# adaLN block on one core: the second part of the modulation vector summed by GpSimd during units 8 to 11

## The chip, the cores and the metric

The kernel runs on one core of a Trainium2 chip. A core has TensorE (matmuls, in the profile PE, its weight loads PEld), VectorE (DVE), ScalarE (ACT), GpSimd (POOL) and SyncE (SP, which here only issues DMAs); each works through its own queue of instructions in order, and they wait for each other by semaphores. SBUF is the on-chip memory of 128 partitions, PSUM the memory that TensorE writes to. The metric is the device time of one execution in microseconds (us).

## The reference

One transformer block with adaptive layer norm: 2048 tokens of width 448, 16 heads of 28, an MLP of 1792. A vector of six times 448 numbers, the modulation, is computed from the condition c and scales and shifts the two layer norms and the two branches:

```python
x = A_x
mod = (_silu(c) @ w_mod).reshape(c.shape[0], 6, 1, -1)
sa, ca, ga, sb, cb, gb = (mod[:, 0], mod[:, 1], mod[:, 2], mod[:, 3], mod[:, 4], mod[:, 5])
h = _layernorm(x, axis=-1) * (1 + ca) + sa
x = x + ga * _A_ref(h, A_wqkv, A_wo)      # softmax attention over 16 heads
h = _layernorm(x, axis=-1) * (1 + cb) + sb
x = x + gb * _B_ref(h, B_w1, B_b1, B_w2, B_b2)   # layer norm, GELU MLP
```

sa and ca are needed at once, for the first layer norm. The other four, ga, sb, cb and gb (called the second part of the modulation here), are needed late: ga scales the output weights of the attention, cb and sb the second layer norm, gb the MLP's second weights and its bias b2.

## The kernel before

Everything is float32; matmuls that must be exact are made of products of a high and a low half in the fp32r type. The work goes in three stages.

**First phase.** Blocks of 512 tokens (b = 0 to 3) go through the layer norm, transposes and the products for q, k and v. For each block a list of tasks runs (the loop at L830, index n within block b): q and k by groups of four heads, then v. Beside the tasks the kernel computes the row maxima of the scores that softmax needs: one matmul into a PSUM tile and one VectorE reduction over 512 columns each (`max_one`, the reduction at L481). The second part of the modulation stands in this phase. `mod_load` loads a chunk k of w_mod's rows (k = 0 to 2 of 128 rows, k = 3 of 64), 1792 columns wide, to the slots v2 and v3: k 0 and 1 in block 0, task 6, k 2 and 3 in block 1, tasks 0 and 1. `mod_mm` (block 1, tasks 0 to 3) multiplies it on TensorE by the silu of c: four matmuls per k, one for each 448 columns, each with 32 output rows that are all alike. `mod_fin` copies the four results out of PSUM (ScalarE, one of the copies adds 1 for cb), writes them to DRAM and loads them back, spread over all partitions, as the four rows `rows["ga"]`, `"sb"`, `"cb"` and `"gb"`.

**Second phase: 16 units of 16 steps.** A unit is one group g of four heads and one block qt of 512 queries (u = 4 g + qt, so units 8 to 11 are group 2); a step is 128 keys. The loop at L1311 writes the order of every engine's instructions out by hand. A step has twelve score matmuls (L1348) in two halves, two exponentials on ScalarE (L1361), four matmuls of probabilities by values (`av`, L1303), and beside them the row maxima of a later group. From step 121 on (`RING`) three PSUM tiles for scores go round, and the maxima of a step are one single, in the only tile left for it (m1, reduction L481), and one pair, in the score tile that is just unused (reduction L686). At the end of a step whatever the table `sched` holds for it is issued: `at(step, fn)` appends to a list, so what was put in earlier is issued earlier.

After each unit, `unit_end_tasks` divides its result by the softmax sums. For a unit u with base = 16 (u + 1) and the tasks marked `staged` (all that matter here): `t_den` at base + 1 (a DMA), `t_rec` at base + 4 (VectorE's reciprocal, a DMA to DRAM and a DMA back, spread over partitions, to the tile osb), `t_split` at base + 10 (GpSimd multiplies, L1061) and `t_split2` at base + 11 (VectorE casts the high half, L1071, GpSimd subtracts the low half, L1072, and eight DMAs store both). The tuple `times` has these offsets counted from base + 1. At each unit's third step `load_q` fetches the queries of the next unit; `load_hi` fetches q and k of a later group for the maxima, and `put` stores the maxima of a unit into its queries (L528). All of these DMAs stand in one queue, SyncE's.

In unit 0 `wo_prep` prepares the attention's output weights: it loads five pieces (`wo_item`), GpSimd multiplies each by `rows["ga"]`, VectorE casts the high half (L986, L981) and GpSimd subtracts. b2 is loaded at step 15 and multiplied by `rows["gb"]` at step 28. The results are first used by the projections in steps 8 to 11 of units 13 and 14.

**Third stage.** The MLP, with the second layer norm inside.

The names that the change touches: `cst` (a small tile of constants), `mod_load`, `mod_mm`, `mod_fin`, `wo_item`'s `rest` (the second half of a piece, put into `sched`), and the entries of `sched` for `wo_prep` and b2. The slots a2h, a3h and b1h are halves of larger slots that are free in the second phase until attention results are loaded into them at the end of unit 12 (`load_o`).

Of the kernel before, what the change touches and what calls it, by code (L numbers as in the profile page):

```python
# [13 lines left out]
F32 = mybir.dt.float32  # L14
F32R = mybir.dt.float32r
AF = mybir.ActivationFunctionType
ALU = mybir.AluOpType
# [15 lines left out]
P1RATE = 4  # L33
LAST_MAX = NKT - 4
RING = 121
PAIR_AT = (2, 2, 0, 2)
PAIR_ROWS = {(0, 2): 2, (0, 3): 3, (1, 0): 2, (1, 1): 2, (1, 2): 3}
WO_MAX = 3
# [6 lines left out]
def tile_adaln_block(ctx: ExitStack, tc: tile.TileContext, x, wqkv, wo, w1, b1, w2, b2, c, w_mod, out):  # L45
# [33 lines left out]
    def sbt(tag, shape, dt=F32, bufs=1):  # L79
        return sb.tile(shape, dt, tag=tag, name=nm(tag), bufs=bufs)  # L80

    def slot(tag, shape, dt=F32R):
        return sb.tile(shape, dt, tag="slot_" + tag, name=nm("slot_" + tag), bufs=1)
# [28 lines left out]
    def ps_o():  # L112
        return ps_tile("o")
# [7 lines left out]

    ident = sbt("ident", [128, 128])
    make_identity(nc, ident)
    cst = sbt("cst", [128, 5])
    neg_half, zero_col = cst[:, 0:4], cst[:, 4:5]
    pool.memset(neg_half, -0.5)
    pool.memset(zero_col, 0.0)


    cols = sbt("cols", [128, 2 * NC])  # L130
# [178 lines left out]
    def warm_up(n):  # L309
        for _ in range(n):  # L310
            pe.matmul(warm[:, :128], ident, ident, start=True, stop=True)
# [2 lines left out]
    pc = ps_o()  # L314
    pe.transpose(pc[:, :NC], c_rows, ident[:NC, :NC])
    act.activation(sil_b, pc[:, :NC, None].broadcast_to([128, NC, 32]), AF.Silu)
    warm_up(5)
    for k in range(NC):
        for j in range(2):
# [418 lines left out]

    mod = {}

    def mod_load(k):
        mod[k] = slot(f"v{2 + k % 2}", [128, 4 * D], F32)
        load_mod(mod[k], k, 2 * D, 4)

    def mod_mm(k):
        if k == 0:
            mod["p"] = ps_o()
        p = mod["p"]
        for j in range(4):
            rs_, cs = mod_part(k, j, 4)  # L750
            pe.matmul(
                p[32 * j : 32 * j + 32, :D], sil_b[rs_, k, :], mod[k][rs_, cs],
                start=(k == 0), stop=(k == NC - 1),
            )

    def mod_fin():
        t = sbt("full", [128, 512], bufs=3)
        act.copy(t[0:64, :D], mod["p"][0:64, :D])
        act.activation(t[64:96, :D], mod["p"][64:96, :D], AF.Identity, bias=1.0)
        act.copy(t[96:128, :D], mod["p"][96:128, :D])  # L760
        sp.dma_start(drow, t[0:128:32, :D])
        for j, name in enumerate(("ga", "sb", "cb", "gb")):
            t = sbt("row_" + ("b2g" if name == "ga" else name), [128, D])
            sp.dma_start(t, drow[j][None].broadcast_to([128, D]))
            rows[name] = t
# [51 lines left out]
    for b in range(NB):  # L817
# [12 lines left out]
        for n, (tb, kind, g) in enumerate(tasks):  # L830
# [41 lines left out]
                    later[n - 7](None)  # L872
            if n == (4 if b else 6):
                v_init(b)
            if b == 0 and n == 6:
                mod_load(0)
                mod_load(1)
            if b == 1 and n == 8:
                put_last_rows()
            if b == 2 and n == 5:  # L880
                sp.dma_start(b1_col, b1.rearrange("(k p) -> p k", p=128))
            if b == 1:
                if n < 2:
                    mod_mm(n)
                    mod_load(2 + n)
                elif n in (2, 3):
                    mod_mm(n)
                    if n == 3:
                        mod_fin()
            if not more:  # L890
                if n == 0:
                    load_q(0)
# [68 lines left out]
    def wo_item(n):  # L961
        def ld(r):
            if n == 4:
                pool.memset(r[:, :D], 0.0)
                for j in range(4):
                    sp.dma_start(r[32 * j : 32 * j + DH, :D], wo[NP + DH * j : NP + DH * j + DH, :])
                return
            p0 = 0
            for r0, r1 in (((128 * n, 128 * n + 128),), MIX_HI, MIX_LO)[max(0, n - 1)]:
                sp.dma_start(r[p0 : p0 + r1 - r0, :D], wo[r0:r1, :])  # L970
                p0 += r1 - r0

        def go(r):
            full = sbt("full", [128, 512], bufs=3)
            ps = slice(0, 112 if n == 3 else 128)
            pool.tensor_tensor(out=full[ps, :D], in0=r[ps, :D], in1=rows["ga"][ps], op=ALU.mult)

            def rest():
                if n == 3:
                    hi = sbt("hi", [128, 512], F32R, bufs=3)  # L980
                    dve.tensor_copy(hi[ps, :D], full[ps, :D])  # L981
                    pool.tensor_tensor(out=wo_p[1][ps, 2, :], in0=full[ps, :D], in1=f(hi)[ps, :D], op=ALU.subtract)
                    pool.tensor_copy(wo_p[1][0:32, 2, :], f(hi)[0:32, :D])
                    return
                k = min(n, 3)
                dve.tensor_copy(wo_p[0][:, k, :], full[:, :D])  # L986
                if n != 2:
                    pool.tensor_tensor(out=wo_p[1][:, k, :], in0=full[:, :D], in1=f(wo_p[0])[:, k, :], op=ALU.subtract)

            at(6 + 2 * n, rest)  # L990

        return ld, go

# [224 lines left out]
        sched.setdefault(step, []).append(fn)  # L1218

    wo_prep = Prep([wo_item(n) for n in range(5)])  # L1220
    at(0, lambda: wo_prep.load(2))
    for n in range(5):
        at(4 + 2 * n, wo_prep.step)

    def b2_load():
        rows["b2"] = raw_t()
# [13 lines left out]
        at(1 + i, lambda: put_spare(1))  # L1240
    for g in (1, 2):
        at(6 + g, lambda g=g: put_ones(g))
    at(15, b2_load)
    at(28, b2_mul)
    last0 = NKT * (NU - 1)
    lnst = [ln2_stages(b) for b in range(NB)]
    for i in range(14):
# [257 lines left out]
```

## Time and profile before

| | |
|---|---|
| time, median of 3 runs | 1103.45 us (1102.35 to 1103.99) |
| time of the profiled execution | 1103.82 us |
| its span, first to last instruction | 1101.7 us |
| granted TensorE clock | 1.00 |
| DMA | 82.67 MB, mean 75 GB/s |

In the profiled execution the first phase takes the time until about 167 us, the 16 units go on until about 792 us, and the MLP fills the rest. Steps of the second phase take some 2.3 us each from step 121 on. A row of an engine in order of time reads: start and length in us, engine, line, operation, output<-inputs, shape, how many were merged, and in brackets how long the engine was idle before and what ended that. A grouped row has line, engine, operation, shapes, count, then busy us and mean ns. "28*128" before a matmul's shape is rows and columns of TensorE's array in use. fp32 matmuls of `mod_mm` and `av` appear as two records each.

### The profile page before, as it was taken

The numbers are of one execution on the slowest core, as the hardware profiler recorded it, in microseconds if no ns is written. First come the engines' busy times: TensorE is split into PE (matmuls) and PEld (weight loads), VectorE is DVE, ScalarE is ACT, GpSimd is POOL, SyncE is SP. The second block draws the span as 40 slices with busy tenths as digits, with TensorE's granted clock in tenths as the row PEclk, the third lists the DMA queues.
The fourth block names the chain that finished last, engine by engine and source line by source line (L and its number), as shares of the span: only waits on it lengthen the run. The fifth ranks groups of instructions, "written<-read, shape, count | busy, mean of one in ns | idle before, by whom it ended". The sixth has DMA issues, their size and how long they took to land.

```text
span 1101.7 us, 20731 instructions
## 1 busy us (share of the span) xinstructions
PE 1094.3 (99%) x8303; PEld 665.3 (60%) x8303; DVE 798.9 (73%) x1382; ACT 697.3 (63%) x883; POOL 196.8 (18%) x201
## 2 busy tenths in 40 slices
PE   9999999999999999999999999999999999999998
PEld 6756675444444444444444444554488888888887
DVE  6968788999999989988888888574655644444322
ACT  4655667888888888888888888678933411211210
POOL 1543332210000000000000000116123214023000
PEclk9999999999999999999999999999999999999999
DMA  9553354221222201231211313111451000000000
GB/s 311 199 191 106 99 183 138 60 64 33 75 76 61 76 28 40 69 102 47 69 48 38 98 42 99 57 31 59 146 144 50 27 34 1 15 20 1 34 1 34
DMA packets 51094, 82.67 MB, mean 75 GB/s; under 512 B 13327, under 2 KB 19878, under 8 KB 50986
## 3 DMA queue, kind: packets, MB, share of 16 engines
q1 hardware_dynamic: 50514, 80.61, 23.9%
q8 instruction: 65, 1.06, 0.4%
q10 hardware_dynamic: 148, 0.46, 0.1%
q0 software_dynamic: 336, 0.28, 0.1%
q14 instruction: 31, 0.25, 0.1%
HBM read 56.25 MB, written 26.75 MB: 75 GB/s over the span
## 4 chain that ended last, share of the span: by engine, by line
PE 97%; DVE 1%; ACT 0%; DMA 0%; issue 0%; ACTq 0%; DVEq 0%
PE s L1348 23%; PE o L1303 23%; PE m L396 17%; PE pa L396 9%; PE m L476 8%; PE s L1439 3%; PE s L1440 3%; PE s L1438 3%; PE s L476 2%; PE t L1439 1%; PE t L1440 1%; PE t L1438 1%; PE o L277 1%; DVE mxp L481 0%; PE ma L476 0%; PE m L277 0%
## 5 line engine op out<-in xcount | busy, mean ns | idle before, releaser
L481 DVE TENSOR_REDUCE mxp<-m 128x1 f32<-128x512 f32 x555 | 359.9, 686 | 64.7 <-PE m L476 46.9
L1348 PE MATMUL s<-slot_b,slot_a 28*128 28x512 f32 (+1 forms) x3072 | 356.7, 423 | 0.0
L1348 PEld LDWEIGHTS s<-slot_b,slot_a 28*128 28x128 f32 (+1 forms) x3072 | 211.2, 183 | 175.8 <-ACT slot_c L1361 96.4
L476 PE MATMUL m<-kh,qh 28*128 28x512 f32 x607 | 227.0, 468 | 0.4 <-DVE mxp L481 0.3
L1361 ACT ACTIVATE slot_c<-s 128x1024 f32<-128x1024 f32 x170 | 174.8, 1028 | 51.5 <-PE s L1348 50.8
L1303 PE MATMUL o<-slot_c,v 128*32 128x512 f32 x680 | 178.9, 605 | 0.0
L1394 ACT ACTIVATE full<-m,b_col 128x512 f32<-128x512 f32 x56 | 38.6, 689 | 205.3 <-PE m L396 188.5
L686 DVE TENSOR_REDUCE mxp<-s 128x2 f32<-128x1024 f32 x107 | 131.2, 1226 | 5.0
L1303 PE MATMUL o<-slot_c1h,v 128*32 128x512 f32 x512 | 134.7, 605 | 0.0
L1303 PE MATMUL o<-slot_c0h,v 128*32 128x512 f32 x508 | 133.6, 605 | 0.0
L1361 ACT ACTIVATE slot_c1h<-s 128x1024 f32<-128x1024 f32 x128 | 130.7, 1021 | 0.0
L1361 ACT ACTIVATE slot_c0h<-s 128x1024 f32<-128x1024 f32 x127 | 130.5, 1027 | 0.0
L1397 DVE CAST hi<-full 128x512 fp32r<-128x512 f32 x42 | 18.6, 443 | 121.1 <-ACT full L1394 121.1
L1361 ACT ACTIVATE slot_d<-s 128x1024 f32<-128x1024 f32 x86 | 88.4, 1028 | 25.2 <-PE s L1348 24.9
L476 PEld LDWEIGHTS m<-kh,qh 28*128 28x128 f32 x607 | 90.8, 182 | 15.2 <-DVE mxp L481 13.3
L1303 PE MATMUL o<-slot_d,v 128*32 128x512 f32 x344 | 90.5, 605 | 0.4 <-ACT osb L1267 0.4
L1061 POOL TENSOR_TENSOR osb<-osb,osb 128x512 f32<-128x512 f32 x16 | 20.6, 1284 | 363.5 <-DMA osb<-drec 247.1
L1398 DVE TENSOR_TENSOR lo<-full,hi 128x512 fp32r<-128x512 f32 x56 | 43.0, 768 | 26.6 <-ACT hi L1397 22.6
L396 PE MATMUL m<-y,slot_a 128*128 128x512 f32 x160 | 60.7, 395 | 0.0
L481 DVE TENSOR_REDUCE mxp<-ma 128x1 f32<-128x512 f32 x61 | 39.5, 682 | 13.2 <-PE m L476 8.0
L1303 PEld LDWEIGHTS o<-slot_c,v 128*32 128x32 f32 x680 | 24.5, 108 | 39.0 <-issue 36.4
L650 DVE CUSTOM_DVE_ANT_0 slot_d0i<-m,slot_d0i 128x512 f32<-128x512 f32 x54 | 37.3, 691 | 14.3 <-PE m L476 11.6
(351 smaller groups left out, 1835.7 us busy)
## 6 DMA issues: line engine op xcount, KB each, us to landing
slot_b<-d SPq DMA_DIRECT2D x32, 256.0 KB
slot_a<-d SPq DMA_DIRECT2D x32, 256.0 KB
d<-lo SPq DMA_DIRECT2D x28, 256.0 KB
d<-hi SPq DMA_DIRECT2D x16, 256.0 KB
osb<-drec SPq DMA_DIRECT2D x15, 256.0 KB
out_dram<-xn SPq DMA_DIRECT2D x16, 224.0 KB
raw<-in_B_w_dram SPq DMA_DIRECT2D x14, 224.0 KB
qh<-d SPq DMA_DIRECT2D x12, 256.0 KB
```

What stands on the lines that cost most here:

```text
L396: pe.matmul(p, a, b, start=(i == 0), stop=(i == len(terms) - 1))
L476: pe.matmul(m, qh_sb[(g, qt)][js, i * 128 : (i + 1) * 128], k[js, :], start=True, stop=True)
L481: dve.tensor_reduce(out=mxp[(g, qt)][:, i, j, cch : cch + 1], in_=m, op=ALU.max, axis=AX.X)
L686: dve.tensor_reduce(out=mxp[(g, qt)][:, i, j : j + 2, cch], in_=t, op=ALU.max, axis=AX.X)
L1303: pe.matmul(o[32 * j : 32 * j + 32, :], v_sb[kt // 4][:, kt % 4, 4 * g + j, :], p[j // 2][:, j % 2, :], start=(kt == 0), stop=(kt == NKT - 1),
L1348: pe.matmul(s2[:, jj, :], ks[rows_, kp, kc], qs[rows_, qp, :], start=(term == 0), stop=(term == 2))
L1361: act.activation(pt[hf], s2, AF.Exp, scale=SCALE)
L1394: act.activation(gf, p, AF.Gelu_apprx_tanh, bias=b1_col[:, i : i + 1])
L1398: dve.tensor_tensor(out=glo, in0=gf, in1=f(ghi), op=ALU.subtract)
L1438: pe.matmul(pp, ghi[:, ts], w_hi, start=(m == 0), stop=False)
L1439: pe.matmul(pp, ghi[:, ts], w_lo, start=False, stop=False)
L1440: pe.matmul(pp, glo[:, ts], w_hi, start=False, stop=(m == NFT - 1))
```

## The change

The second part of the modulation is no longer computed in the first phase. It is cut into two halves h of 896 columns (ga and sb; cb and gb). From step 130 on, every third step, one chunk k of one half is loaded to the slot a2h, which is the only buffer; two steps later GpSimd multiplies it by the column of silu(c) that belongs to its rows, and adds it to a running total (b1h for the first half, a3h for the second) unless it is the first. So there are eight loads, eight products and six additions, at steps 130 to 153. At step 156 the new `mod_fin` adds each total over the partitions by four matmuls with a weight of ones, taken from the ones column that v_sb holds anyway, copies the result out of PSUM in one ScalarE instruction whose bias `third` adds 1 on partitions 64 to 95 (cb), and goes on as before through DRAM. The rows that were in units 0 and 1 and need ga or gb move: the output weights to steps 162 to 176, b2's load to 177 and its product to 190.

```diff
+MOD_AT = 130
+WO_AT = 166
...
-    cst = sbt("cst", [128, 5])
-    neg_half, zero_col = cst[:, 0:4], cst[:, 4:5]
+    cst = sbt("cst", [128, 6])
+    neg_half, zero_col, third = cst[:, 0:4], cst[:, 4:5], cst[:, 5:6]
     pool.memset(neg_half, -0.5)
-    pool.memset(zero_col, 0.0)
+    pool.memset(cst[:, 4:6], 0.0)
+    pool.memset(third[64:96], 1.0)
+    sil_c = sbt("sil_c", [128, NC])
...
     act.activation(sil_b, pc[:, :NC, None].broadcast_to([128, NC, 32]), AF.Silu)
+    act.activation(sil_c, pc[:, :NC], AF.Silu)
...
-    def mod_load(k):
-        mod[k] = slot(f"v{2 + k % 2}", [128, 4 * D], F32)
-        load_mod(mod[k], k, 2 * D, 4)
-
-    def mod_mm(k):
+    def mod_rows(h, k):
+        return slice(0, 128) if k < 3 else slice(64 * h, 64 * h + 64)
+
+    def mod_load(h, k):
+        rs_ = mod_rows(h, k)
+        mod["raw"] = slot("a2h", [128, 2 * D], F32)
+        c0 = 2 * D * (1 + h)
+        sp.dma_start(mod["raw"][rs_], w_mod[128 * k : min(128 * k + 128, D), c0 : c0 + 2 * D])
+
+    def mod_add(h, k):
+        rs_ = mod_rows(h, k)
         if k == 0:
-            mod["p"] = ps_o()
-        p = mod["p"]
+            mod[h] = slot(("b1h", "a3h")[h], [128, 2 * D], F32)
+        raw, total = mod["raw"][rs_], mod[h][rs_]
+        col = sil_c[rs_, k : k + 1].broadcast_to([rs_.stop - rs_.start, 2 * D])
+        pool.tensor_tensor(out=raw if k else total, in0=raw, in1=col, op=ALU.mult)
+        if k:
+            pool.tensor_tensor(out=total, in0=total, in1=raw, op=ALU.add)
+
+    def mod_fin():
+        p = ps_mx()
+        ones_ = v_sb[0].rearrange("p t h d -> p (t h) d")[:, 0:32, DH]
         for j in range(4):
-            rs_, cs = mod_part(k, j, 4)
             pe.matmul(
-                p[32 * j : 32 * j + 32, :D], sil_b[rs_, k, :], mod[k][rs_, cs],
-                start=(k == 0), stop=(k == NC - 1),
+                p[32 * j : 32 * j + 32, :D], ones_, mod[j // 2][:, j % 2 * D : (j % 2 + 1) * D], start=True, stop=True,
             )
-
-    def mod_fin():
         t = sbt("full", [128, 512], bufs=3)
-        act.copy(t[0:64, :D], mod["p"][0:64, :D])
-        act.activation(t[64:96, :D], mod["p"][64:96, :D], AF.Identity, bias=1.0)
-        act.copy(t[96:128, :D], mod["p"][96:128, :D])
+        act.activation(t[:, :D], p[:, :D], AF.Identity, bias=third)
         sp.dma_start(drow, t[0:128:32, :D])
...
-            if b == 0 and n == 6:
-                mod_load(0)
-                mod_load(1)
...
-            if b == 1:
-                if n < 2:
-                    mod_mm(n)
-                    mod_load(2 + n)
-                elif n in (2, 3):
-                    mod_mm(n)
-                    if n == 3:
-                        mod_fin()
...
-            at(6 + 2 * n, rest)
+            at(WO_AT + 2 + 2 * n, rest)
...
-    at(0, lambda: wo_prep.load(2))
+    for i in range(2 * NC):
+        h, k = divmod(i, NC)
+        at(MOD_AT + 3 * i, lambda h=h, k=k: mod_load(h, k))
+        at(MOD_AT + 3 * i + 2, lambda h=h, k=k: mod_add(h, k))
+    at(MOD_AT + 6 * NC + 2, mod_fin)
+    at(WO_AT - 4, lambda: wo_prep.load(2))
     for n in range(5):
-        at(4 + 2 * n, wo_prep.step)
+        at(WO_AT + 2 * n, wo_prep.step)
...
-    at(15, b2_load)
-    at(28, b2_mul)
+    at(WO_AT + 11, b2_load)
+    at(WO_AT + 24, b2_mul)
```

## The prediction

> **What bounds the kernel now.** I read the page first (busy time, the chain that ended last), then the busy time of stretches, then the engines in order of time around each place that the change touches.
>
> ```profile
> PE 1094.3 (99%) x8303; PEld 665.3 (60%) x8303; DVE 798.9 (73%) x1382; ACT 697.3 (63%) x883; POOL 196.8 (18%) x201
> ...
> PE 97%; DVE 1%; ACT 0%; DMA 0%; issue 0%; ACTq 0%; DVEq 0%
> ```
>
> TensorE is busy 99% of the span and holds 97% of the chain. So a matmul taken out is worth its time, unless another engine is close behind, and any wait that TensorE newly meets is paid in full. GpSimd, at 18%, looks free. The stretches show who is close behind (the columns are the length, then PE, PEld, DVE, ACT, POOL busy):
>
> ```profile
> 65.00:75.00 10.00, 10.00 (x55) 5.52 (x54) 7.18 (x15) 5.70 (x12) 2.57 (x2) 1.00 0.82 274
> 520.00:560.00 40.00, 40.00 (x414) 17.16 (x410) 35.00 (x41) 34.80 (x38) 2.58 (x2) 1.00 0.21 59
> ```
>
> In the first phase, where matmuls leave, VectorE has 2.8 us of 10 to spare. In units 8 and 9 it has only 5 of 40, an eighth: VectorE there can't be late by much before TensorE is. The granted clock is 1.00 in both.
>
> **Removed: the first phase's matmuls.** TensorE in order of time, at the first and the last of the four calls of `mod_mm`:
>
> ```profile
> 58.34 0.96 PE L751 MATMUL o<-slot_v,slot_d 128*32 128x448 f32 x8
> 59.23 1.20 PE L396 MATMUL pa<-slot_c,slot_a 128*128 128x512 f32 x4
> ...
> 72.94 0.96 PE L751 MATMUL o<-slot_v,slot_d 64*32 64x448 f32 x8
> 73.82 1.20 PE L396 MATMUL pa<-slot_c,slot_a 128*128 128x512 f32 x4
> ```
>
> The next matmul starts 0.89 us after the first of a call, so the four hold TensorE for 4 x 0.89 = 3.55 us. How much comes back depends on VectorE, whose idle times there are the brackets:
>
> ```profile
> 61.12 1.89 DVE L481 TENSOR_REDUCE mxp<-m 128x1 f32<-128x512 f32 x3 [5.10 <-PE ma L476]
> ...
> 67.70 0.69 DVE L481 TENSOR_REDUCE mxp<-ma 128x1 f32<-128x512 f32 x1 [2.30 <-PE m L476]
> ...
> 70.56 1.29 DVE L481 TENSOR_REDUCE mxp<-ma 128x1 f32<-128x512 f32 x2 [0.37 <-PE m L476]
> ...
> 77.12 0.69 DVE L481 TENSOR_REDUCE mxp<-m 128x1 f32<-128x512 f32 x1 [2.27 <-PE ma L476]
> ```
>
> One idle time is only 0.37 us, less than the 0.89 taken out ahead of it; there TensorE waits about 0.5 us for a PSUM tile. The others are long enough. I take **-3.0 us**; ends -3.55 and, if VectorE's backlog takes it all, 0. ScalarE's three copies out of PSUM and SyncE's five DMAs of the old `mod_fin` go too. ScalarE is busy 5.70 us in 10 and nothing waited for those rows, so they count nothing.
>
> **Added at the start.** The small Silu for `sil_c` follows L316 on ScalarE. Its next instruction comes after an idle time that hides a fraction of a microsecond, so nothing:
>
> ```profile
> 8.34 0.76 ACT L233 ACTIVATE xn<-acc,nm,rs 128x448 f32<-128x448 f32 x1 [2.26 <-POOL nm L249]
> ```
>
> **Added: the new `mod_fin` at step 156.** Four fp32 matmuls of the form that L751 had, 0.89 us on TensorE. They take the PSUM tile m1, the only one for single maxima in these units, and hand it back when ScalarE has copied it out. Step 156 ends on TensorE with the L1303 row at 552.65, step 157 begins at 553.18:
>
> ```profile
> 75.08 0.54 ACT L759 ACTIVATE full<-o 32x448 f32<-32x448 f32 x1
> ...
> 552.84 1.02 ACT L1361 ACTIVATE slot_c0h<-s 128x1024 f32<-128x1024 f32 x1
> 554.18 1.02 ACT L1361 ACTIVATE slot_c<-s 128x1024 f32<-128x1024 f32 x1 [0.33 <-PE s L1348]
> ...
> 552.65 0.60 PE L1303 MATMUL o<-slot_c,v 128*32 128x512 f32 x2
> 553.18 0.50 PE L1348 MATMUL s<-slot_b,slot_a 29*128 29x512 f32 x2
> ```
>
> The matmuls would run from 553.2 to 554.1, the copy (0.54) from about 554.2 to 554.7. Step 157's single maximum, wanted right after its first scores at 554.3, waits until 554.7: 0.5 us. Together **+1.4 us**; ends 0.9 (matmuls alone) and 1.5.
>
> **Added: the sum on GpSimd, and the queue it stands in.** This is the term that decides. Each k needs a load into the single buffer a2h, a product and (for k > 0) an addition; the next load waits for that. Load, product, addition, load run strictly one after another, while three steps are set aside for each. I need two durations. GpSimd:
>
> ```profile
> 506.65 1.29 POOL L1061 TENSOR_TENSOR osb<-osb,osb 128x512 f32<-128x512 f32 x1 [25.65 <-ACT slot_c1h L1361]
> ...
> 542.22 1.29 POOL L1061 TENSOR_TENSOR osb<-osb,osb 128x512 f32<-128x512 f32 x1 [25.30 <-DMA osb<-drec]
> ...
> 691.03 1.15 POOL L1036 TENSOR_TENSOR acc<-acc,full 128x448 f32<-128x448 f32 x1 [2.72 <-ACT full L1035]
> ```
>
> 1.15 us for 448 columns and 1.29 for 512 make 0.13 to 0.14 us for 64 more; for 896 columns 1.29 + 6 x 0.13 = 2.06 us (an estimate from these rows). Half the partitions (k = 3) save nothing by L286:
>
> ```profile
> L286 POOL TENSOR_TENSOR slot_c0h<-full,slot_c0h 64x512 fp32r<-64x512 f32 x2 | 2.6, 1284 | 4.2 <-ACT slot_c0h L282 4.2
> ...
> L983 POOL CAST slot_e<-hi 32x448 fp32r<-32x448 f32 x1 | 0.5, 546 | 0.1
> ```
>
> The second factor of the product is one column repeated, which no row shows; a one-input cast (0.55 for 448, so 1.1 for 896) is the lower end, 2.06 the value, since both forms name two inputs. The transfer:
>
> ```profile
> 62.05 0.43 SPq L161 DMA_DIRECT2D slot_v<-in_w_mod_dram  x1
> ...
> 67.79 0.16 PEld L751 LDWEIGHTS o<-slot_v,slot_d 128*32 128x32 f32 x8 [0.37 <-DMA slot_v<-in_w_mod_dram]
> ...
> 492.00 0.95 SPq L774 DMA_DIRECT2D slot_b<-d  x2
> 495.51 2.27 SPq L528 DMA_DIRECT2D slot_b<-full  x4
> 499.79 0.33 SPq L1054 DMA_DIRECT2D drec<-den  x1
> 501.41 0.56 SPq L1056 DMA_DIRECT2D osb<-drec  x1
> ...
> 515.53 1.92 SPq L1082 DMA_DIRECT2D o<-hi  x4
> ```
>
> 896 KB took 5.7 us (62.05 until TensorE's wait for it ends), 256 KB 3.5 (492.00 until the DMA that waits for it goes at 495.51). For 448 KB a line between gives 4.2; both had other transfers beside them, so I take 4.0, and 3.4 for the 224 KB of k = 3; ends 3.5 and 5.7.
>
> Now the order. The first load goes behind `load_q` at 493.0. The second (h 0, k 1, step 133) stands on SyncE's queue behind `t_rec` of unit 7 (step 132), whose reload of `osb` is issued at 501.41 to 501.97. That reload lands at 506.65 (the division on GpSimd starts then; the next unit's also starts 5 us after its issue, with the DMA named). So the second load is issued at 502.0 and lands about 506.7: product and addition until 510.8. Third load 510.9 to 514.9, GpSimd until 519.0. Only behind that comes unit 7's `t_split` on GpSimd's queue (step 138; now it runs at 506.65), until 520.3. VectorE's cast of `t_split2` needs it:
>
> ```profile
> 515.09 0.42 DVE L1071 CAST hi<-osb 128x512 fp32r<-128x512 f32 x1
> 515.55 0.69 DVE L481 TENSOR_REDUCE mxp<-m 128x1 f32<-128x512 f32 x1
> 516.22 1.23 DVE L686 TENSOR_REDUCE mxp<-s 128x2 f32<-128x1024 f32 x1
> 517.70 0.69 DVE L481 TENSOR_REDUCE mxp<-m 128x1 f32<-128x512 f32 x1 [0.25 <-PE s L1348]
> ...
> 551.15 0.42 DVE L1071 CAST hi<-osb 128x512 fp32r<-128x512 f32 x1
> ...
> 517.12 0.50 PE L1348 MATMUL s<-slot_b,slot_a 29*128 29x512 f32 x2
> 517.98 0.50 PE L476 MATMUL s<-kh,qh 28*128 28x512 f32 x2
> ```
>
> The cast starts at 515.09 now and would wait 5.2 us. Behind it stand the reductions that give m1 and the pair's tile back. The pair's reduction ends at 517.45, TensorE writes that tile again before 517.98: slack 0.4. So TensorE stands for 4.8 us.
>
> From there everything is 4.8 later, and GpSimd's chain goes on from 519.0: k 3 with 3.4 + 4.1 until 526.6, the next half's k 0 (4.0 + 2.1) until 532.8, k 1 541.0, k 2 549.2, k 3 556.8 (0.1 for each hand-over), then unit 8's division until 558.2. Its cast, now at 551.15, is due at 555.95: 2.2 late, less 0.4, 1.8 us more. `mod_fin` comes after that and finds the sums ready. **+6.6 us** for both stops. Lower end: loads of 3.5, the second one not held by the reload, and products of 1.1: unit 7's division ends at 516.8, 1.7 late, +1.3 us and no second stop. Upper end: 5.7 for a load, 1.7 more for each of four and half of that for two of k = 3, +15.1; that row moved twice the bytes, so I let the range reach to loads of 4.7, +10.0.
>
> **Moved: the output weights' preparation and b2**, from unit 0 to steps 162 to 190.
>
> ```profile
> L986 DVE CAST slot_e<-full x4: 382/383/384, 186.7 to 206.8; 128x448 fp32r<-128x448 f32 x4
> ```
>
> Five casts of 0.38 on VectorE, GpSimd's products (1.15 each) and eleven loads on SyncE. In unit 0 TensorE gains nothing measurable. At the new place the cast of L1071 (0.42) sits in a step whose next reduction still starts on time (515.55) with 0.25 idle soon after; a cast a step apart is covered in the same way. Without that cover it would cost 5 x 0.38 = 1.9 us. The users, the projections, come after step 208. I count 0.
>
> **Sum**: -3.0 + 1.4 + 6.6 = +5.0 us on a span of 1101.7; the profiled execution took 1103.82, so 1108.8. The median of the runs shown, 1103.45, lies 0.37 below it: **1108.5 us**.
>
> **Rivals.** (1) *GpSimd keeps ahead, no stop.* It decides at unit 7's division: that must end by 515.5, so from 502.0, less 1.4 for the division, two loads, two products and two additions fit in 12.1 us. Products and additions at 2.06 leave 1.9 us for each load, below any row; with cheap products (1.1) 2.9, still below 3.5. For it speaks that GpSimd is idle nearly throughout. Then -3.0 + 1.4 = -1.6, 1101.9; with the whole 3.55 back and 0.9 for `mod_fin`, 1100.8. (2) *VectorE eats the first phase's gain* (the 0.37 row spreads): 0 instead of -3.0, 1111.5; against it stand idle times of 2.3 us on both sides. (3) *GpSimd's long instructions hold VectorE's short ones up.*
>
> ```profile
> L217 DVE TENSOR_SCALAR xn<-acc,mv,rs x18: 472/506/1316, 8.9 to 991.3; 128x448 f32<-128x448 f32 x18
> ```
>
> Instructions of this one form run 506 ns in the middle and 1316 at most, so something holds single ones, and GpSimd is the engine that the change loads. A hold of up to 2.06 - 0.4 = 1.7 us for each of the two units' reciprocals, and 1.15 - 0.4 = 0.75 for each of the five moved casts, makes 7.1; with GpSimd busy about half of that time some 3, so 1111.5. Against it: the L986 row has all its four casts at 382 to 384 ns, with GpSimd's products in the same steps of unit 0. The Trainium skill (SBUF — State Buffer, "Who interferes with whom") states that GpSimd and VectorE's two-port modes exclude each other for a whole instruction, casts among them, and that `tensor_reduce` never contends on this chip. By that rule only the five casts would pay, 3.8 us at most, 1112.2; the spread of the L217 row fits it.
>
> **From these to the numbers.** Forecast 0.62 (of it 0.10 with stops so short that the time stays within 0.2%); rival 1 0.15, of it 0.09 faster; rival 2 0.11; rival 3 0.12. About 0.2%, 2.2 us, is what a measurement of this kernel can tell from no change. Faster 0.09, same 0.16, slower 0.75. The range goes from 1102.0 (below the short stop's sum, -3.0 + 1.4 + 1.3 = -0.3 or 1103.2, and about at rival 1's 1101.9) to 1113.0 (above the long stop's, -3.0 + 1.4 + 10.0 = +8.4 or 1111.9, and above rivals 2 and 3).
>
> **What would show it.** In the first phase: no L751, and the 0.37 us gone. At unit 7's division: GpSimd some 13 us later than its reload allows, VectorE's cast of the first unit waiting for GpSimd by about 5 us with TensorE's step at the same length longer, and a shorter stop one unit on. Loads on SyncE named as waiting for GpSimd. Wrong would be casts that start without waiting, a product well under 2 us, or `t_split` ahead of the third addition.

## The result and the profile after

The changed kernel takes 1111.08 us (median of 4 runs, 1110.66 to 1112.34) against 1103.61 us before (median of 4 runs, 1102.35 to 1103.99): the ratio is 1.0072, with an interval of 1.0056 to 1.0088. It is 7.5 us slower; 1108.5 was forecast. The profiled execution took 1110.66 us with a span of 1108.9.

The page of the changed kernel: busy time, granted clock and GB/s in 40 slices, and the chain that ended last.

```profile
PE 1094.7 (99%) x8279; PEld 665.3 (60%) x8279; DVE 798.7 (72%) x1382; ACT 696.6 (63%) x882; POOL 222.6 (20%) x216
...
PEclk9999999999999999998999999999999999999999
...
PE 92%; DMA 3%; POOL 2%; DVE 1%; issue 1%; ACT 0%; SPq 0%; POOLq 0%; DVEq 0%; ACTq 0%
```

24 matmul records fewer, and yet PE is busy 0.4 us longer. The chain, 97% TensorE before, now has DMAs and GpSimd in it. And the clock's row has an 8 in slice 19, counted from 1, which lies at 499 to 527 us. The before kernel had no such place.

To find where the time went, I take the start of the same step in both kernels. Before, in order of time on TensorE (the first scores of steps 144, 156 and 158; step 141's, 517.12, stands in the prediction):

```profile
523.85 0.50 PE L1348 MATMUL s<-slot_b,slot_a 29*128 29x512 f32 x2
...
550.91 0.50 PE L1348 MATMUL s<-slot_b,slot_a 29*128 29x512 f32 x2
...
555.34 0.50 PE L1348 MATMUL s<-slot_b,slot_a 29*128 29x512 f32 x2
```

After, rows of all engines in order of time around unit 7's division (steps 133 to 144) and unit 8's (156 to 158), and between them the load of the second half's k 1 with its product:

```profile
498.68 9.97 SPq L753 DMA_DIRECT2D slot_a2h<-in_w_mod_dram  x2
504.42 1.68 POOL L761 TENSOR_TENSOR slot_a2h<-slot_a2h,sil_c 128x896 f32<-128x896 f32 x1 [5.77 <-DMA slot_a2h<-in_w_mod_dram]
511.84 1.68 POOL L761 TENSOR_TENSOR slot_a2h<-slot_a2h,sil_c 128x896 f32<-128x896 f32 x1 [3.54 <-DMA slot_a2h<-in_w_mod_dram]
512.70 0.50 PE L1355 MATMUL s<-slot_b,slot_a 29*128 29x512 f32 x2
515.62 1.26 POOL L1063 TENSOR_TENSOR osb<-osb,osb 128x512 f32<-128x512 f32 x1
516.92 0.43 DVE L1073 CAST hi<-osb 128x512 fp32r<-128x512 f32 x1 [6.17 <-POOL osb L1063]
518.00 0.79 PE L481 MATMUL m<-kh,qh 28*128 28x512 f32 x1 [4.80 <-DVE mxp L486]
528.75 0.50 PE L1355 MATMUL s<-slot_b,slot_a 29*128 29x512 f32 x2
532.75 0.37 SPq L753 DMA_DIRECT2D slot_a2h<-in_w_mod_dram  x1
537.43 1.68 POOL L761 TENSOR_TENSOR slot_a2h<-slot_a2h,sil_c 128x896 f32<-128x896 f32 x1 [9.60 <-DMA slot_a2h<-in_w_mod_dram]
...
555.83 0.50 PE L1355 MATMUL s<-slot_b,slot_a 29*128 29x512 f32 x2
557.50 0.43 DVE L1073 CAST hi<-osb 128x512 fp32r<-128x512 f32 x1 [1.34 <-POOL osb L1063]
558.67 0.62 PE L769 MATMUL m<-slot_b1h,v 128*32 128x448 f32 x2 [0.50 <-DVE mxp L486]
560.43 0.49 PE L481 MATMUL m<-kh,qh 28*128 28x512 f32 x1 [0.31 <-ACT full L773]
562.54 0.49 PE L1355 MATMUL s<-slot_b,slot_a 29*128 29x512 f32 x2
```

The chain reads from the top: the load for k 1, issued at 498.68, lands at 504.42; product and addition follow; the next load lands at 511.84; product and addition again; and only then, at 515.62, the division of unit 7 (L1063), which stands behind that addition on GpSimd's queue. VectorE's cast stood 6.17 us for it, and TensorE 4.80 us for the reductions behind the cast.

From step 141 to 144 the changed kernel needs 528.75 - 512.70 = 16.05 us, the one before 523.85 - 517.12 = 6.73: **9.3 us more**, of which 4.80 are the wait. The rest shows in the stretches of the changed kernel (length; PE, PEld, DVE, ACT, POOL busy; then the granted clock, DMA share and GB/s), cut where the clock changed:

```profile
513.20:516.61 3.41, 0.00 (x0) 0.00 (x0) 0.00 (x0) 0.29 (x1) 3.33 (x3) 1.00 0.02 5
516.61:520.03 3.42, 2.03 (x11) 1.30 (x13) 2.76 (x4) 0.77 (x1) 2.58 (x3) 0.50 0.53 141
520.03:523.44 3.41, 3.41 (x20) 1.02 (x22) 1.23 (x1) 1.28 (x2) 2.72 (x2) 0.50 0.25 61
523.44:526.85 3.41, 3.41 (x23) 1.02 (x23) 1.92 (x2) 1.94 (x2) 0.70 (x1) 0.50 0.46 135
526.85:530.27 3.42, 3.42 (x42) 1.63 (x42) 2.69 (x4) 2.45 (x3) 0.98 (x1) 1.00 0.00 0
```

After a stretch in which TensorE did nothing, its clock is 0.50 for 10.24 us: 20 and 23 matmuls in a stretch that otherwise holds 42. From 518.00, when TensorE goes on, to 526.85 are 8.85 us at half speed with TensorE busy throughout, about 4.4 us lost (half of it, an estimate). That and the wait make up the 9.3 to within 0.1. (The expectations below, written earlier, divide it as 5.3 and 4.1: 5.3 is the time from the start of step 141, 512.70, to 518.00, with 0.50 us of matmuls in it.)

From step 156 to 158 it is (562.54 - 555.83) - (555.34 - 550.91) = 2.3 us for the second stop and the new `mod_fin` together. One more place follows: step 174 takes 2.73 us instead of 2.27. VectorE and GpSimd there:

```profile
595.95 1.17 POOL L978 TENSOR_TENSOR full<-raw,row_b2g 112x448 f32<-112x448 f32 x1
...
596.35 1.09 DVE L988 CAST slot_e<-full 128x448 fp32r<-128x448 f32 x1
```

A moved cast of the output weights took 1.09 us instead of the 0.38 of before (L986 in the prediction): it began 0.40 after a product of GpSimd did, and ended 0.32 after that product's end. The theory for the experiments: two stops from GpSimd's queue, a half clock that the first one brings on, and small prices for `mod_fin` and held casts, against a gain in the first phase. The rivals: GpSimd's work itself disturbs the others wherever it stands; the transfers are at fault, not the order; the half clock has to do with something else.

### The profile page after: what moved, and what is told of

Same layout as the page of the kernel before. It is cut to its first block, busy times and chain, and to the rows that moved or that the text cites. A ratio compares the mean times of both kernels' runs of the same rounds, so it can differ in the third digit from the quotient of the medians.

```text
span 1108.9 us, 20699 instructions
## 1 busy us (share of the span) xinstructions
PE 1094.7 (99%) x8279; PEld 665.3 (60%) x8279; DVE 798.7 (72%) x1382; ACT 696.6 (63%) x882; POOL 222.6 (20%) x216
## 4 chain that ended last, share of the span: by engine, by line
PE 92%; DMA 3%; POOL 2%; DVE 1%; issue 1%; ACT 0%; SPq 0%; POOLq 0%; DVEq 0%; ACTq 0%
PE s L1355 21%; PE o L1310 21%; PE m L401 17%; PE pa L401 9%; PE m L481 8%; PE s L1446 3%; PE s L1447 3%; PE s L1445 3%; DMA slot_a2h<-in_w_mod_dram 2%; PE s L481 1%; PE t L1446 1%; PE t L1447 1%; PE t L1445 1%; POOL slot_a2h L761 1%; PE o L281 1%; DVE mxp L486 1%
## 5 line engine op out<-in xcount | busy, mean ns | idle before, releaser
L1063 POOL TENSOR_TENSOR osb<-osb,osb 128x512 f32<-128x512 f32 x16 | 20.5, 1283 | 308.8 <-DMA osb<-drec 289.4
L401 PE MATMUL m<-y,slot_a 128*128 128x512 f32 x160 | 60.6, 395 | 0.0
```

The costliest lines, as they stand in the source:

```text
L401: pe.matmul(p, a, b, start=(i == 0), stop=(i == len(terms) - 1))
```

## The experiments

**The order on GpSimd's queue.** The third chunk's product and addition go behind unit 7's division, everything of the later chunks two steps later, `mod_fin` to step 160.

```diff
-        at(MOD_AT + 3 * i, lambda h=h, k=k: mod_load(h, k))
-        at(MOD_AT + 3 * i + 2, lambda h=h, k=k: mod_add(h, k))
-    at(MOD_AT + 6 * NC + 2, mod_fin)
+        late_ = 2 if i > 2 else 0
+        at(MOD_AT + 3 * i + late_, lambda h=h, k=k: mod_load(h, k))
+        at(MOD_AT + 3 * i + (2 if i > 1 else 0) + 2, lambda h=h, k=k: mod_add(h, k))
+    at(MOD_AT + 6 * NC + 6, mod_fin)
```

> The work of the change is all there; only its place in GpSimd's queue moves: the third chunk's product and addition go from step 138 to step 140, behind unit 7's division and low half, everything after that two steps later, and the partition sums from step 156 to 160. Theory (VectorE's cast waits because unit 7's and unit 8's divisions stand behind the chain of loads, products and additions on GpSimd's queue): no stop at steps 141 and 156, no half clock, so 1103.6 - 3.5 (first phase) + 1.4 (partition sums) + 0.4 (a cast held once) = about 1102. Rival (GpSimd's added work or the added DMA traffic itself holds VectorE or TensorE in these units, wherever it stands): the steps from 130 to 155 stay long and the time stays above 1106.

Measured: 1104.71 us (11 runs, 1103.20 to 1107.93), ratio 1.0021 with 1.0012 to 1.0030. In order of time:

```profile
511.40 0.42 DVE L1073 CAST hi<-osb 128x512 fp32r<-128x512 f32 x1
...
548.99 1.28 POOL L1063 TENSOR_TENSOR osb<-osb,osb 128x512 f32<-128x512 f32 x1
550.29 0.43 DVE L1073 CAST hi<-osb 128x512 fp32r<-128x512 f32 x1 [2.74 <-POOL osb L1063]
551.38 0.50 PE L481 MATMUL m<-kh,qh 28*128 28x512 f32 x1 [1.38 <-DVE mxp L486]
```

The first stop is gone whole: unit 7's cast waits for nothing. The second remains, since the chain of load, product and addition is still running when unit 8's division is due. So order decides the first stop, as predicted, but two steps of room aren't enough for the second, and 1102 was missed. Here a wait of 1.38 us and one of 0.40 right after it were followed by the half clock:

```profile
549.77:553.18 3.41, 1.64 (x15) 0.78 (x13) 2.75 (x4) 1.44 (x2) 1.18 (x2) 1.00 0.50 135
553.18:556.60 3.42, 3.42 (x24) 1.25 (x23) 1.55 (x2) 1.03 (x1) 3.26 (x3) 0.50 0.02 5
```

This is the profiled execution (1106.60 us, its clock 0.998 on average). Of the eleven executions, the five with a clock of 0.999 or 1.000 took 1103.20 to 1104.12 us, the six with 0.996 to 0.998 took 1104.71 to 1107.93. So the clock falls in some executions of the same kernel and not in others. What decides it is not shown, since a trace shows only one of them: a longer stop is one candidate, another place of the stop in the clock's stretches (last section) the other. And the held cast is dearer here: two of the moved casts took 1.29 and 1.14 us, and steps 172 to 174 grow by 1.5 us together.

**The first stop filled with matmuls.** 22 matmuls over 28 rows, into the score tile that is written next:

```diff
+                if step == 141 and n == 0:
+                    for _ in range(22):
+                        pe.matmul(s2[:, 0, :], ks[64 * hf : 64 * hf + DH, 0, kc], qs[64 * hf : 64 * hf + DH, 0, :], start=True, stop=True)
```

> The changed kernel with 22 more matmuls on TensorE ahead of step 141's scores (28 rows by 512 columns, 0.23 us each, their results are overwritten), which fill the time in which TensorE stands there. Theory (of the 9.4 us that steps 141 to 143 grew by, 5.3 are the wait and 4.1 are half clock that follows because TensorE stood idle): the wait stays, the clock stays at 1.00, steps 141 to 143 grow by about 5.3 in all, 1111.1 - 4.1 = about 1107. Rival (the half clock has another cause, for instance the load of all engines starting together): the clock still halves and the time is 1111 or more.

Measured: 1111.14 us (4 runs, 1110.66 to 1112.05), ratio 1.0077: a miss. The stretches, cut at the change of clock:

```profile
516.01:519.42 3.41, 3.37 (x16) 2.33 (x14) 0.88 (x2) 0.00 (x0) 2.87 (x3) 1.00 0.19 47
519.42:522.83 3.41, 3.21 (x17) 1.53 (x21) 2.67 (x4) 1.35 (x2) 2.85 (x3) 0.50 0.53 138
```

PE is busy 3.37 of 3.41 us, and the clock falls all the same. So the busy column isn't what the clock goes by; the stops with different fills, below, take this up.

**Without the additions.** The six additions are left out, so the four rows hold the first chunk's share alone.

```diff
-        if k:
-            pool.tensor_tensor(out=total, in0=total, in1=raw, op=ALU.add)
```

> Leaves out the six additions of the running totals, so that a chain link is a load and a product alone; the queue's order stays. Unit 7's division then ends 2 x 2.1 us sooner, some 2 us after VectorE is ready for its cast. Theory: a first stop of about 1.6 us and no second one, 1103.6 - 3.5 + 1.6 + 1.4 + 0.4 = about 1103.5 if so short a stop leaves the clock at 1.00; about 4 more, 1107.5, if any stop halves it for 10 us. Rival (what delays is the number of DMAs and not GpSimd's part of the chain): the stop stays above 4 us.

Measured: 1104.18 us (10 runs, 1103.44 to 1106.92), ratio 1.0017 with 1.0008 to 1.0026. In the profiled execution (1103.49 us) the first stop costs 2.1 us by the step starts and the clock stays at 1.00; there is no second stop; steps 156 to 158, with `mod_fin` in them, are 1.44 us longer than before. So 2.1 us fewer per addition on GpSimd decide between a long and a short stop. In that execution the short one costs no more than its length. It may not do so each time: four of the ten executions kept the clock at 1.000 (1103.44 to 1103.80 us), in the six others it was 0.996 to 0.998 on average and they took 1103.93 to 1106.92. No trace shows one of these.

**Two buffers.** Every second chunk goes to d0h and d0i instead of a2h, so that its load doesn't wait for the product of the one before; products and additions are done in halves of 448 columns:

```diff
-        mod["raw"] = slot("a2h", [128, 2 * D], F32)
...
+        if k % 2:
+            mod["raw", h, k] = [slot(f"d0{x}", [128, 1, 512], F32)[:, 0, :D] for x in "hi"]
+        else:
+            t = slot("a2h", [128, 2 * D], F32)
+            mod["raw", h, k] = [t[:, :D], t[:, D:]]
```

> The changed kernel with a second buffer for the loaded chunks (odd chunks in two free halves of 448 columns, so that their load goes out while the even one is worked on; their products and additions are two of 448 columns). Steps and queue order stay. Theory (the chain is late because load, product, addition, load run one after another in one buffer): GpSimd reaches unit 7's division about 5 us sooner, before VectorE needs it, no stops, about 1102. Rival (the chain is late for GpSimd's 27 us of work alone): the stops stay, above 1107.

Measured: 1108.42 us (5 runs, 1107.46 to 1111.96), ratio 1.0057 with 1.0043 to 1.0071: a miss. In order of time:

```profile
497.97 0.55 SPq L1067 DMA_DIRECT2D osb<-drec  x1
...
504.55 0.93 POOL L770 TENSOR_TENSOR slot_d0h<-slot_d0h,sil_c 128x448 f32<-128x448 f32 x1 [5.54 <-DMA slot_d0h<-in_w_mod_dram]
...
512.99 1.28 POOL L1072 TENSOR_TENSOR osb<-osb,osb 128x512 f32<-128x512 f32 x1
514.30 0.43 DVE L1082 CAST hi<-osb 128x512 fp32r<-128x512 f32 x1 [3.79 <-POOL osb L1072]
```

The second chunk's load still stands behind `t_rec`'s reload (497.97) and lands only at 504.5, as it did with one buffer. From there GpSimd alone needs 8.4 us for two chunks (504.55 to 512.99). The buffer cost 2.6 us (the division began at 515.62 in the changed kernel), not the whole lateness: the place behind the reload and GpSimd's own work are enough for a stop.

**The chunks set apart.** Two buffers, and no new work ahead of any division: the first half's chunks in steps 140 to 150, behind unit 7's split and before unit 8's, the second half's 16 steps later, then `mod_fin` and the output weights.

```diff
-MOD_AT = 130
-WO_AT = 166
+MOD_AT = 140
+WO_AT = 182
...
+        at(MOD_AT + 16 * h + (0, 1, 5, 8)[k], lambda h=h, k=k: mod_load(h, k))
+        at(MOD_AT + 16 * h + (3, 5, 8, 10)[k], lambda h=h, k=k: mod_add(h, k))
+    at(MOD_AT + 28, mod_fin)
```

> Keeps the change, but puts the four chunks of the first half between unit 7's split (step 139) and unit 8's (step 154), the four of the second half between unit 8's (155) and unit 9's (170), every second chunk in a buffer of its own, mod_fin at step 168 and the preparation of wo 16 steps later than the changed kernel has it. Nothing of GpSimd's new work then stands ahead of a t_split on its queue. Theory of the queue: no stop, clock 1.00 throughout, and what is left is the first phase (-3.5, from the step starts of the runs so far), the end of the sum (+1.4) and one held cast (+0.4): 1102.8 - 1.7 = 1101.1 us. Rival, GpSimd's work holds VectorE or ScalarE wherever it stands, or the loads hold SP's other transfers: a stop remains or the steps from 141 to 168 grow one by one, 1103 us or more.

Measured: 1101.36 us (11 runs, 1100.59 to 1102.07) against 1103.50 (15 runs), ratio 0.9982 with 0.9973 to 0.9991: faster than both kernels. The clock is 1.00 throughout, no step from 141 to 167 grows, steps 168 and 169 (`mod_fin`) grow by 1.43 us together, step 190 by 0.65. GpSimd does all that it did in the changed kernel, so its work as such isn't what made that one slow; where it stands is.

**The casts kept apart.** The version before this one, with the output weights' preparation behind unit 10's split and each cast one step after its product, not beside the next product:

```diff
-WO_AT = 182
+WO_AT = 188
...
-            at(WO_AT + 2 + 2 * n, rest)
+            at(WO_AT + 1 + 2 * n, rest)
```

> The version with the chunks set apart, with one thing more: wo's preparation starts at step 188, behind unit 10's split, and each of its casts on VectorE comes one step after its product on GpSimd instead of two, and so not beside the next product. In the version before it one such cast took 1.04 us beside a running product and step 190 grew by 0.66. Theory that the cast is held by the product beside it: every one of these casts takes 0.4 us, no step from 186 on grows, 0.6 us less, 1100.7 us. Rival, GpSimd's products cost the chain the same wherever the casts stand: 1101.4 us.

Measured: 1100.90 us (11 runs, 1099.95 to 1101.47) against 1103.04 (20 runs), ratio 0.9982 with 0.9973 to 0.9990. The casts as one group, min/median/max in ns, first in the chunks set apart:

```profile
L997 DVE CAST slot_e<-full x4: 384/416/1043, 613.9 to 632.4; 128x448 fp32r<-128x448 f32 x4
```

and then with the casts kept apart:

```profile
L997 DVE CAST slot_e<-full x4: 382/383/384, 624.2 to 642.2; 128x448 fp32r<-128x448 f32 x4
```

The held cast is gone and no step grows from 186 on. The 0.46 us between the two medians show nothing: the kernel before, measured beside each, differs by as much (1103.50 and 1103.04), and the ratios are the same. So the price of the held cast rests on the step starts of the traces, and the rival's time is not excluded.

**Without most of the first phase's matmuls.** In the kernel before, twelve of the sixteen:

```diff
-                start=(k == 0), stop=(k == NC - 1),
+                start=True, stop=True,
...
-                    mod_mm(n)
+                    if n == 0:
+                        mod_mm(0)
                     mod_load(2 + n)
                 elif n in (2, 3):
-                    mod_mm(n)
```

> The kernel before without twelve of the sixteen matmuls of the second part of the modulation (those of the last three chunks of rows; their share is missing from the four rows, the loads and the rest stay). It has nothing of GpSimd's new work. If the first phase pays 3.5 us for sixteen, as the step starts of the changed kernels say, twelve are worth 2.6 us: 1103.3 - 2.6 = 1100.7 us. If VectorE or the buffers hold the phase there and the earlier start came from elsewhere, 1103 us.

Measured: 1100.44 us (10 runs, 1100.04 to 1101.28) against 1103.04, ratio 0.9976 with 0.9967 to 0.9985: 2.6 us, so 3.5 for all sixteen in proportion. In its trace step 0 starts 2.3 us earlier than before, which would make 3.1. VectorE doesn't eat the gain.

**Stops of six lengths.** In the kernel before, TensorE is made to wait for a chain on GpSimd:

```diff
+STOPS = (0, 256, 512, 768, 1280, 1792)
...
+        pool.tensor_copy(t[:, :8], pend[2][pend[1] % 2 if ring else 1][:, 0, :8])
+        for i in range(n // 896 + 1):
+            w = min(896, n - 896 * i)
+            if w:
+                pool.tensor_tensor(out=t[:, :w], in0=t[:, :w], in1=t[:, :w], op=ALU.mult)
+        p = ps_mx()
...
+        pe.matmul(p[0:8, 0:8], t[:, 0:8], t[:, 0:8], start=True, stop=True)
```

> The kernel before with six artificial stops of TensorE, 13 steps apart: at steps 133, 146, 159, 172, 185 and 198 a tiny matmul waits for a chain on GpSimd that starts from the step's exponentials and is 0, 256, 512, 768, 1280 and 1792 columns longer (about 0.6 us more for each 256). Nothing else of the change is in it, and the result of the kernel is the same. Theory that idle time of TensorE alone halves the clock: the short stops (under about 2 us) leave the clock at 1.00, the long ones (over about 3.4 us) are each followed by some 7 to 10 us at 0.50 and cost 3 to 4 us more than the wait. Rival, the half clock belongs to the change's own GpSimd work or to the particular place: no stop is followed by 0.50, and each costs just its wait.

Measured: 1117.16 us, one run. The first chain was too short to stop anything; the others:

```profile
531.22 0.20 PE L1248 MATMUL m<-slot_a2h 128*8 128x8 f32 x2 [0.76 <-POOL m L518]
561.82 0.20 PE L1248 MATMUL m<-slot_a2h 128*8 128x8 f32 x2 [1.13 <-POOL slot_a2h L1239]
592.91 0.20 PE L1248 MATMUL m<-slot_a2h 128*8 128x8 f32 x2 [1.55 <-POOL m L518]
624.94 0.20 PE L1248 MATMUL m<-slot_a2h 128*8 128x8 f32 x2 [2.65 <-POOL slot_a2h L1239]
659.47 0.20 PE L1248 MATMUL m<-slot_a2h 128*8 128x8 f32 x2 [3.65 <-POOL slot_a2h L1239]
```

By the step starts they cost 1.2, 1.4, 1.8, 4.4 and 5.4 us. Up to 1.55 that is the wait and 0.2 to 0.4 beside it. From 2.65 on it is the wait and 1.7: behind each of the last two the clock is 0.50 for 3.4 us (625.9 to 629.3, 660.0 to 663.4). So idle time of TensorE alone halves the clock in this execution, with none of the change's work in the kernel. A half clock of 3.4 us costs 1.7 - 0.3 = 1.4, and three such stretches 4.2, about what the changed kernel lost (4.4). The expected 7 to 10 us at 0.50 were too long for these stops.

**Stops of one length, filled.** The same chain of 1792 columns four times: empty, with 20 matmuls of 28 rows, with 40 of 128 rows on 32 columns, with 20 on the whole array.

```diff
+FILLS = (None, ("one", 20), ("cols", 40), ("full", 20))
...
+            if fill[0] == "cols":
+                pe.matmul(p[32 * (i % 4) : 32 * (i % 4) + 32, :D], f(wo_p[0])[:, 0, 0:32], f(wo_p[0])[:, 1, :], start=True, stop=True)
+            else:
+                r = slice(0, DH if fill[0] == "one" else 128)
+                pe.matmul(p[:, :D], wa[r], wb[r], start=True, stop=True)
```

> The kernel before with four stops of the same length (GpSimd chain of 1792 columns, about 5 us) at steps 133, 153, 173 and 193: the first empty, the second filled with 20 matmuls over 28 rows, the third with 40 of four bytes on 32 columns each in turn, the fourth with 20 over all 128 rows and columns. If the clock follows how long TensorE is idle, only the first is followed by 0.50. If it follows how much of the array works, as the kernel with 22 single matmuls of 28 rows in its stop suggests, the first and the second are, and the fourth is not.

Measured: 1128.60 us, one run. The stretches, on the grid of 3.41 us on which this execution's clock changed, two for each stop (one within it, and the next):

```profile
500.16:503.58 3.42, 0.30 (x4) 0.00 (x0) 0.39 (x1) 0.72 (x1) 3.26 (x3) 1.00 0.16 58
503.58:506.99 3.41, 3.12 (x22) 1.78 (x25) 1.56 (x2) 1.29 (x2) 1.51 (x2) 0.50 0.07 23
...
551.37:554.78 3.41, 3.41 (x20) 2.88 (x17) 0.39 (x1) 0.85 (x1) 3.25 (x3) 1.00 0.01 4
554.78:558.19 3.41, 3.41 (x20) 2.69 (x21) 0.41 (x1) 0.00 (x0) 1.52 (x2) 0.50 0.00 0
...
605.98:609.39 3.41, 3.41 (x42) 1.17 (x36) 0.00 (x0) 0.00 (x0) 1.35 (x1) 1.00 0.03 5
609.39:612.80 3.41, 3.41 (x41) 1.67 (x37) 0.89 (x2) 0.59 (x1) 0.00 (x0) 1.00 0.00 0
...
657.18:660.60 3.42, 3.42 (x21) 2.81 (x19) 0.00 (x0) 0.00 (x0) 2.55 (x3) 1.00 0.47 143
660.60:664.01 3.41, 3.41 (x41) 1.79 (x40) 2.46 (x3) 2.14 (x3) 0.00 (x0) 1.00 0.02 5
```

The first fill (28 rows) keeps PE busy for the whole stretch, and the clock falls to 0.50 as after the empty stop, for 6.8 us in both. The two others keep it at 1.00. The first and the last fill differ only in the rows in use: 20 matmuls of 28 rows don't hold the clock, 20 of 128 rows do. That fits the second theory, that it goes by how much of the array works, and the changed kernel's stop, where 22 matmuls of 28 rows did not hold the clock either. Filling has its price: by the step starts the four stops cost 6.2, 7.3, 7.5 and 4.4 us. The third fill held the clock but outlasted the wait, and cost more than the empty stop.

**The first stop filled with matmuls that count.** 28 matmuls of 128 rows on 32 columns each, at the same place as the 22 above, in the changed kernel:

```diff
+                if step == 141 and n == 0:
+                    for i in range(28):
+                        pe.matmul(
+                            s2[32 * (i % 4) : 32 * (i % 4) + 32, 0, :], v_sb[0][:, 0, 0, :],
+                            v_sb[1].rearrange("p t h d -> p (t h d)")[:, :512], start=True, stop=True,
+                        )
```

> The changed kernel with its first stop filled: 28 matmuls of 128 rows on 32 columns each, the four groups of columns in turn, ahead of step 141's scores, about 5 us of work that reads v and writes where the scores write next. The wait of 5.3 us stays as it is. Theory that the clock follows how much of the array works, and that the half clock behind the first stop costs about 4.1 us: the clock stays at 1.00 there and the time is 1111.1 - 4.1 = 1107.0 us. Rival, the half clock comes from something else in the change, or costs little: 1111 us.

Measured: 1110.56 us (5 runs, 1109.15 to 1118.23), ratio 1.0068 with 1.0052 to 1.0084: a miss. The profiled execution is the longest of the five, and in it the load of k 1 landed 3.8 us later than in the changed kernel, so it can't be set beside that one. Its stretches:

```profile
516.32:519.73 3.41, 3.41 (x36) 0.91 (x28) 0.00 (x0) 0.00 (x0) 3.33 (x3) 1.00 0.00 0
519.73:523.14 3.41, 1.54 (x15) 0.61 (x13) 2.34 (x4) 0.48 (x1) 2.50 (x3) 1.00 0.43 114
523.14:526.56 3.42, 3.42 (x20) 1.01 (x24) 1.64 (x2) 1.56 (x2) 3.34 (x2) 0.50 0.36 88
```

While the fill ran, the clock held. Then 1.87 us of idle time in the next stretch halved it, as the 1.77 us did in the first experiment. In the four other executions the clock was 0.999 to 1.000 on average, against 0.995 in all four of the changed kernel, so the half clock was as good as gone; yet they took 1109.15 to 1111.58 us. The fill lasts 6.22 us in the trace, 1.4 more than the wait of 4.80 that it was to fill. With 4.4 won and 1.4 spent, 1108.1 would be expected (an estimate), and they lie 1.0 to 3.5 above it; no trace shows where the rest went. So this run doesn't confirm the 4.4 us: that price rests on the changed kernel's own trace and on the artificial stops.

## Why the prediction came out as it did

It was right in direction, in place and in the mechanism of the stops, and 2.6 us low, since its sum has nothing for the half clock. That it came so near is in part luck: errors cancelled under both stops. By its terms:

- **First phase, -3.0**: 3.5 in the changed kernel's trace, where step 0 starts 4.5 us earlier, 1.0 of them start-up; the kernel without twelve matmuls gives 3.1 to 3.5 in proportion. That is near the larger of its two ends. The 0.5 us that was held back for VectorE's short idle time was not needed.
- **First stop, +4.8**: TensorE's wait is 4.80 us. Errors cancelled under it. The second load took 5.7 us (issued at 498.68, product at 504.42) and not the 4.7 it was given there, the next 3.5 and not 4.0, and a product 1.68 and not 2.06; VectorE's cast stood for 6.17 and not 5.2, and the slack behind it was 1.4 and not 0.4. That a product takes well under 2 us was named among the signs of being wrong; it came true without moving the stop. The mechanism is shown: with the order changed the stop is gone, and with the chunks apart both are.
- **Missing: the half clock**, about 4.4 us behind that wait. This is the term that the sum lacks. The prediction counted a stop of TensorE at its length; here the stop of 4.80 us cost 9.3. The clock was read only as 1.00 in the trace of before, which holds no such stop, and the question what a stop does to it wasn't asked. The Trainium skill (TensorE: Matmul & The Clock Gate, section "Part 1: The HAM clock gate (the "warmup" mystery)") does give the rule: half speed after an idle window of about 3.4 us. The length of the window agrees with the traces (3.41); but less idle time was enough here, 1.77 us in one stretch.
- **Second stop and `mod_fin`, +1.8 and +1.4**: 2.3 us together. `mod_fin` alone is 1.43 and 1.44 in the two kernels in which it stands by itself, so the stop is 0.9. VectorE's cast waited 1.34 us where 2.2 was forecast, but not by the path of the sum. The chain did not run through: the load of the second half's k 1 was issued only at 532.75, behind a load of kh on SyncE's queue that waited 9.2 us for TensorE, and GpSimd stood idle for 9.60 us. Counted from the start of step 141, unit 8's division ended 3.7 us later than forecast (44.8 for 41.1) and the cast was due 4.6 us later (43.5 for 38.8), since both waited for TensorE, which the half clock had delayed. That the two nearly cancel is luck.
- **Moved preparation, 0**: 0.46 us, by one held cast. This is the third rival's mechanism, at one of five casts instead of all, and the kernel with the casts apart bears it out: 382 to 384 ns each. The Trainium skill (SBUF — State Buffer, "Who interferes with whom"), cited in the prediction, says that of GpSimd and a VectorE cast in a two-port mode the one that issues second is blocked for the whole instruction of the first. The trace agrees, with a cast that ends 0.32 us after the product beside which it began.

-3.5 + 4.8 + 4.4 + 2.3 + 0.46 = +8.5 us against 7.5 between the medians. In the profiled pair the spans differ by 7.2; 1.0 of the missing 1.3 us is start-up, which the last section shows, and 0.3 stay open. Whether the medians differ by the start-up isn't known.

Of the rivals, the first (GpSimd keeps ahead) fell in the changed kernel, but it is just what the kernel with the chunks apart makes true: 1101.36, where the rival gave 1100.8 to 1101.9. The second fell with the twelve matmuls. The third was right about one cast, worth 0.46 us and not the some 3 that it gave.

## What to carry to other kernels

An engine that is 18% busy still has a queue: before work is given to it, look up which short instruction of the critical chain will stand behind the new long ones, and at what step it is due; the same work was worth -0.2% instead of +0.7% once it stood behind that instruction, with a second buffer. A stop that leaves TensorE idle for about half of a stretch of 3.41 us can cost more than its length, because the clock was halved for one to three such stretches afterwards, and 20 to 22 matmuls of 28 rows didn't prevent it. A fill that does must not outlast the wait. One trace shows one execution: look at the clock of the others too before a short stop is called cheap. After a move, look at casts on VectorE beside GpSimd's instructions: 0.38 us became 1.09 here.

## What the hardware showed that was not expected

**The clock goes in stretches of 3.41 us.** Within one execution all changes of the granted clock lie on one grid of this length. (In the changed kernel the 512.0 us at full clock ahead of its first fall are 150 times 3.4133.) The grid begins elsewhere in each execution: divided by 3.4133, the stretch starts 513.20, 549.77, 516.01 and 500.16 of four traces above leave 1.2, 0.2, 0.6 and 1.8 us. So the same stop can lie in one stretch or be split between two. In the traces here each fall to 0.50, leaving out the one at the very end of the kernels, came at the end of a stretch in which PE was idle 1.77 us or more (from 1.77 and 1.87 in the two stretches shown above to the 3.41 of the changed kernel) or filled with 28-row matmuls. The longest idle time that left it at 1.00 was 1.68 us, at the start-up of the kernel with the chunks apart (7.88 to 11.30, PE busy 1.74 of 3.42). The next was 1.52, at the second stop of the kernel with two buffers:

```profile
552.67:556.08 3.41, 1.89 (x23) 0.59 (x18) 0.85 (x2) 2.13 (x3) 2.76 (x3) 1.00 0.01 2
556.08:559.50 3.42, 2.73 (x27) 1.34 (x31) 2.06 (x4) 1.14 (x2) 0.93 (x1) 1.00 0.51 122
```

What decides whether it stays for one, two or three stretches is open: in the changed kernel a stretch with PE busy throughout (520.03 to 523.44) was followed by another at 0.50.

**Start-up differs by 1 us from one execution to the next.** The same matmul of the first phase, ahead of any removed one, starts at 24.86 us in the trace of before (L396) and at 23.89 in that of the changed kernel (L401). The change doesn't do it: in the twelve traces here that matmul starts between 23.66 and 24.98 us, and three variants that keep the change's first phase have it at 24.79, 24.98 and 24.86 (the order on the queue, the stop filled with 22 matmuls, without the additions).

**A product with a repeated column is shorter on GpSimd than an addition.** For 896 columns it is 1.68 us against 2.07 to 2.12, and neither is shorter on 64 partitions than on 128.
